# A gated linear attention in chunks: queries times, keys over the running product of the decays, instead of seven levels of halves

## The chip, the cores and the metric

The kernel runs on one core of a Trainium2 chip. Its engines are TensorE (PE in the profile; its weight loads are listed as PEld), VectorE (DVE), ScalarE (ACT), GpSimd (POOL) and SyncE (SP, which only issues transfers here). The metric is the device time in microseconds of one execution, lower is better.

## What is computed

A recurrence over 768 steps for 4 batches and 8 heads of dimension 48, and then a mixture of experts (8 experts, 2 for each token) on its output:

```python
state = np.zeros((B, H, D, D))
for t in range(S):
    state = alpha[:, :, t, :, None] * state + np.einsum('bhd,bhe->bhde', k[:, :, t], v[:, :, t])
    y[:, :, t] = np.einsum('bhd,bhde->bhe', q[:, :, t], state)
x = y.transpose(0, 2, 1, 3).reshape(3072, 384)
logits = x @ w_gate + np.log1p(np.exp(x @ w_noise)) * noise      # 3072 x 8
# the two best experts of each token, with softmax weights:
out[token] += weight * (np.maximum(x[token] @ w1[e], 0) @ w2[e])
```

alpha is drawn evenly from 0.8 to 1. All numbers are 32 bits wide.

## The kernel before

The 3072 tokens are 24 chunks of 128 (six chunks for each batch). A chunk's output is q times the state that it inherits, decayed, plus the attention inside the chunk: the score of token t on an earlier token s is the sum over the 48 dimensions of q[t] k[s] times the product of the alphas between them.

The kernel never divides by a product of alphas. It builds the scores by doubling. `gla_prepare` (L184) loads the chunk (a, q, k and v, each 192 KB, on SP's queue, `load_chunk` L141), transposes k, q and alpha on PE (`transposed`, L163), makes the products of the diagonal and multiplies q by alpha. `gla_level` (L202) is then called for L = 1, 2, 4 to 64: the right half of each block of 2L tokens is scored against the whole chunk's keys (`scores`, L169, eight products with 64 columns), a predicated copy on DVE takes the part that belongs to this level into the matrix MT (L212), and q's right halves are multiplied by the left half's total decay (DVE, L222), k's left halves by the right half's (POOL, L224), the other halves copied (ACT, L223 and L225), and the totals of the pairs multiplied (POOL, L227). `gla_finish` (L230) transposes the keys, which by then are decayed to the chunk's end, updates the state, and adds two products, q with the old state (L258) and MT with v (L263). The result y is written to x_rows in device memory (L273, SP's queue) and transposed into xT (L271).

The loop (L345) takes two chunks at a time, and their levels alternate, so that one chunk's products run while the other chunk's operands are made. After the pairs of chunks 0 and 2 it issues, on SP's queue, the clearing of out (eight transfers, L357) and the load of w2 (eight transfers of 1.5 MB, L160). After each three chunks `router` (L279) makes the logits on PE (L283), picks the two experts, ranks the tokens within each expert with two more products (L326, L327) and writes 128 x 6 table entries with six scatters of POOL's queue (L338). All six write the one tensor `table`, and so each waits for the one before.

Then a few small operations on one partition make a plan of 55 tiles of 128 tokens (L366 to L391). The memory of the first stage is closed (L393), and the experts' loop fetches a table row, a matrix w1 and the gathered tokens two tiles ahead (`fetch`, L410) and computes each tile (`ffn`, L424).

The scheduler that builds the program sets the waits between the engines, and may move an instruction ahead of others of its engine that aren't ready. What is queued on an engine runs in that order.

Of the kernel before, what the change touches and what calls it, by code (L numbers as in the profile page):

```python
# [17 lines left out]
def kernel(  # L18
# [21 lines left out]

    nc = tc.nc
# [21 lines left out]

    gla = ctx.enter_context(ExitStack())
# [7 lines left out]
    gc = pool("gc", 1, gla)  # L72
    vp = pool("vp", 4, gla)
    kp = pool("kp", 4, gla)
    qp = pool("qp", 4, gla)
    dp = pool("dp", 2, gla)
    sp = pool("sp", 2, gla)
    xtp = pool("xtp", 2, gla)
    rp = pool("rp", 2, gla)
    ps_sc = pool("ps_sc", 2, gla, space=PS)  # L80
    ps_tp = pool("ps_tp", 2, gla, space=PS)
    ps_y = pool("ps_y", 2, gla, space=PS)
# [5 lines left out]
    masks = {}  # L88
    for L in LEVELS:
        g = C // (2 * L)  # L90
        m = gc.tile([C, g, L], F32, name=f"mask{L}")
        nc.gpsimd.memset(m, 1.0)
        nc.gpsimd.affine_select(out=m, in_=m, pattern=[[-2 * L, g], [0, L]], compare_op=ALU.is_ge, fill=0.0,
                                base=0, channel_multiplier=1)
        nc.gpsimd.affine_select(out=m, in_=m, pattern=[[2 * L, g], [0, L]], compare_op=ALU.is_ge, fill=0.0,
                                base=L - 1, channel_multiplier=-1)
        masks[L] = m.bitcast(U32)[:, None, :, :].to_broadcast([C, NP, g, L])
    mask_diag = ident.bitcast(U32)[:, None, :].to_broadcast([C, NP, C])
# [6 lines left out]
    ones = const.tile([C, C], F32, name="ones")  # L105
    nc.gpsimd.memset(ones, 1.0)
# [16 lines left out]
    nc.scalar.dma_start(out=table.rearrange("(p r) w -> p (r w)", p=C), in_=nothing)  # L123
    zeros = const.tile([C, NT // 8, DM], F32, name="zeros")
    nc.gpsimd.memset(zeros, 0.0)

    NIN = 3
    ins = {x: [gc.tile([C, H, DP], F32, name=f"{x}_in{i}") for i in range(NIN)] for x in "aqk"}
    MTs = [gc.tile([C, 2, NP, C], F32, name=f"MT{i}") for i in range(2)]
    S_bds = [gc.tile([C, NP, 2, D], F32, name=f"S_bd{i}") for i in range(2)]  # L130
    for t in [t for x in "aqk" for t in ins[x]]:
        nc.gpsimd.memset(t[:, :, D:DP], 0.0)
    for t in MTs + S_bds:
        nc.vector.memset(t, 0.0)
# [6 lines left out]
    def load_chunk(n):  # L141
        for x, src in (("a", alpha), ("q", q), ("k", k)):
# [5 lines left out]
    noise = gc.tile([C, NT, E], F32, name="noise")  # L148
    w_r = gc.tile([C, KO, 2, E], F32, name="w_r")
# [13 lines left out]
    def transposed(src, dst, copy):  # L163
        tp = ps_tp.tile([C, NP, C], F32, tag="tp", name="tp")
        for j in range(NP):
            nc.tensor.transpose(tp[:, j, :], src[:, 2 * j:2 * j + 2, :], ident)
        copy(dst, tp)  # L167

    def scores(sc, at, width, kT, qcols):  # L169
        for j in range(NP):  # L170
            for i in range(2):
                r = ds(DP * i, D)
                nc.tensor.matmul(sc[i][:, at + j * width:at + (j + 1) * width], kT[r, j, :], qcols[r, j],  # L173
                                 start=True, stop=True)

    def halves(t, l):
        w = t.rearrange("p j (g h l) -> p j g h l", h=2, l=l)
        return w[:, :, :, 0, :], w[:, :, :, 1, :]

    def flat_halves(t, l):  # L180
# [164 lines left out]
    for n in range(0, NT, 2):  # L345
        pair = {m: gla_prepare(m) for m in (n, n + 1)}
        for L in LEVELS:
            for m, c in pair.items():
                gla_level(m, c, L)
# [137 lines left out]
```

## Time and profile before

| | us |
|---|---|
| median of three runs | 1467.92 (1464.04 to 1469.35) |
| the profiled execution | 1463.86 |
| its span, from the first to the last instruction | 1462.2 |
| PE, DVE, ACT, POOL busy | 1241.1, 394.7, 274.5, 425.4 |
| mean granted clock of PE, of full speed | 0.746 |

The page gives, for each engine, its busy time and, in forty slices of the span (36.6 us each), the busy share in tenths. [...] The queries of the trace that are used below are the groups of instructions by line (busy time, mean of one, and the idle time of the engine in front of them with what ended it), the timeline, and the busy time of each engine in given windows.

### The profile page before, as it was taken

What the parts mean: (1) busy time and instruction counts of PE and PEld (TensorE: products, weight loads), DVE (VectorE), ACT (ScalarE), POOL (GpSimd) and SP (SyncE); (2) the same over time, 40 slices, a digit from 0 to 9 for tenths busy, and PEclk for the clock granted to TensorE, in tenths of its full rate; (3) what the DMA queues carried; (4) which work ended last, traced back from release to release, by engine and by line L of the source; (5) the groups of instructions that cost most, each with busy time, mean ns of one, the idle gap of its engine ahead of it and who ended that gap; (6) DMA issues with size and microseconds to landing.
All of it is one profiled execution on the core that took longest, in us unless ns stands there. A gap on an engine that the chain in (4) does not pass through costs nothing. (4 is left out here: it accounts for less than half of the span.)

```text
span 1462.2 us, 21684 instructions
## 1 busy us (share of the span) xinstructions
PE 1241.1 (85%) x8079; PEld 1071.5 (73%) x8079; DVE 394.7 (27%) x985; ACT 274.5 (19%) x603; POOL 425.4 (29%) x653
## 2 busy tenths in 40 slices
PE   6895697997979979699850999989999989999896
PEld 6784696886968879688750777767777777777775
DVE  5443343525435254352620101010101001010100
ACT  2322231322323223232310010001010000001010
POOL 6221432414334143341502122222222222222221
PEclk8655555555555555555555999999999999999999
DMA  9549020221202112010003445444555555555540
GB/s 232 183 172 108 1 55 11 45 44 12 55 12 44 39 18 54 6 34 12 1 11 121 154 176 186 165 172 169 173 186 191 187 194 181 179 183 178 179 165 20
DMA packets 160966, 157.56 MB, mean 108 GB/s; under 512 B 118341, under 2 KB 132862, under 8 KB 160864
## 3 DMA queue, kind: packets, MB, share of 16 engines
q1 hardware_dynamic: 144736, 127.47, 28.4%
q0 software_dynamic: 12096, 28.39, 6.7%
q8 instruction: 66, 1.08, 0.3%
q10 hardware_dynamic: 4032, 0.33, 0.3%
q14 instruction: 36, 0.29, 0.1%
HBM read 139.77 MB, written 20.50 MB: 110 GB/s over the span
## 5 line engine op out<-in xcount | busy, mean ns | idle before, releaser
L437 PEld LDWEIGHTS h_ps<-xt,w 128*128 128x128 f32 x2640 | 308.5, 196 | 10.1 <-DVE xt L431 2.9
L437 PE MATMUL h_ps<-xt,w 128*128 128x128 f32 x2640 | 311.3, 279 | 1.8 <-DVE xt L431 1.7
L173 PE MATMUL sc<-q_new,k_new 48*128 48x64 f32 x2304 | 268.2, 418 | 42.0 <-POOL k_new L224 41.4
L173 PEld LDWEIGHTS sc<-q_new,k_new 48*128 48x128 f32 x2304 | 257.9, 327 | 53.0 <-POOL k_new L224 44.6
L442 PE MATMUL o_ps<-w,h 128*128 x880 | 292.9, 486 | 0.0
L442 PEld LDWEIGHTS o_ps<-w,h 128*128 128x128 f32 x880 | 163.2, 190 | 101.8
L212 DVE COPY_PREDICATED MT<-mask,sc 128x256 f32<-128x256 uint32 x336 | 154.3, 524 | 167.1 <-PE sc L173 164.9
L448 DVE SCALAR_TENSOR_TENSOR o<-o_ps,tab,prev 128x384 f32<-128x384 f32 x55 | 34.0, 618 | 559.7 <-PE o_ps L442 496.3
L439 ACT ACTIVATE h<-h_ps 128x512 f32<-128x512 f32 x110 | 65.7, 597 | 626.7 <-PE h_ps L437 626.7
L449 POOL DMA_INDIRECT out_dram<-o,tab x55 | 56.4, 1026 | 306.7 <-DVE o L448 294.4
L227 POOL TENSOR_TENSOR tot<-tot 128x256 f32<-128x256 f32 (+6 forms) x168 | 59.5, 354 | 216.6 <-ACT tot L167 205.7
L224 POOL TENSOR_TENSOR k_new<-k_new,tot 128x256 f32<-128x256 f32 x144 | 96.3, 683 | 55.3 <-PE sc L173 54.4
L338 POOL DMA_INDIRECT table<-entry,place_u x48 | 48.7, 1015 | 176.9 <-DMA table<-entry,place_u 106.2
L225 ACT COPY k_new<-k_new 128x256 f32<-128x256 f32 x144 | 58.8, 409 | 219.3 <-POOL k_new L224 122.0
L429 PE MATMUL x_ps<-ident,x_in 128*128 128x128 f32 x165 | 28.9, 287 | 81.8 <-DMA x_in<-x_rows,tab 81.8
L429 PEld LDWEIGHTS x_ps<-ident,x_in 128*128 128x128 f32 x165 | 19.7, 144 | 96.3 <-DMA x_in<-x_rows,tab 87.8
L444 POOL DMA_INDIRECT prev<-out_dram,tab x55 | 56.4, 1026 | 112.3 <-DMA out_dram<-o,tab 108.6
L173 PE MATMUL sc<-q,k 48*128 48x128 f32 (+1 forms) x768 | 79.7, 333 | 10.4 <-DVE MT L196 8.7
L173 PEld LDWEIGHTS sc<-q,k 48*128 48x128 f32 x768 | 70.5, 236 | 19.7 <-DVE MT L196 10.2
L263 PEld LDWEIGHTS y<-vt,MT 128*128 128x128 f32 x384 | 83.3, 328 | 0.0
L263 PE MATMUL y<-vt,MT 128*128 128x48 f32 x384 | 83.2, 403 | 0.0
L419 POOL DMA_INDIRECT x_in<-x_rows,tab x55 | 54.8, 996 | 79.4 <-DMA tab<-table 59.8
(107 smaller groups left out, 896.8 us busy)
## 6 DMA issues: line engine op xcount, KB each, us to landing
w<-in_moe_w_dram SPq DMA_DIRECT2D x63, 1536.0 KB, 7.2
a_in<-in_alpha_dram SPq DMA_DIRECT2D x24, 192.0 KB, 3.5
q_in<-in_q_dram SPq DMA_DIRECT2D x24, 192.0 KB, 4.4
k_in<-in_k_dram SPq DMA_DIRECT2D x24, 192.0 KB, 3.3
vt<-in_v_dram SPq DMA_DIRECT2D x24, 192.0 KB, 2.9
out_dram<-zeros SPq DMA_DIRECT2D x8, 576.0 KB, 6.1
x_rows<-y_sb SPq DMA_DIRECT2D x24, 192.0 KB, 2.7
tab<-table SPq DMA_DIRECT2D x55, 1.0 KB, 1.7
```

The lines of the kernel that those rows point to most:

```text
L173: nc.tensor.matmul(sc[i][:, at + j * width:at + (j + 1) * width], kT[r, j, :], qcols[r, j], start=True, stop=True)
L212: nc.vector.copy_predicated(halves(MTs[n % 2][:, i], L)[1], masks[L], part)
L224: nc.gpsimd.tensor_tensor(kl_new, k_left, t_right.to_broadcast([C, NP * g, L]), op=ALU.mult)
L225: nc.scalar.copy(kr_new, k_right)
L227: nc.gpsimd.tensor_tensor(tot_new.rearrange("p j g -> p (j g)")[:, :, None], t_left, t_right, op=ALU.mult)
L263: nc.tensor.matmul(y[:, h, :], MT[:, i, j, :], vt[:, h, :], start=first and h == 0, stop=h == H - 1, skip_group_check=True)
L419: nc.gpsimd.indirect_dma_start(out=x_in[i % NB], out_offset=None, in_=x_rows, in_offset=bass.IndirectOffsetOnAxis(ap=tab[:, 0:1], axis=0), ...
L437: nc.tensor.matmul(h_ps[:, fo, :], w1[:, a, ds((half * FO // 2 + fo) * C, C)], xt[:, a, :], start=a == 0, stop=a == KO - 1)
L439: nc.scalar.activation(h[:, ds(half * FO // 2, FO // 2), :], h_ps, AF.Relu)
L442: nc.tensor.matmul(o_ps, h[:, fo, :], w2[:, ds(e, 1), fo, :].rearrange("p o d -> p (o d)"), start=fo == 0, stop=fo == FO - 1)
L444: nc.gpsimd.indirect_dma_start(out=prev[i % 2], out_offset=None, in_=out, in_offset=bass.IndirectOffsetOnAxis(ap=tab[:, 0:1], axis=0), bou ...
L449: nc.gpsimd.indirect_dma_start(out=out, out_offset=bass.IndirectOffsetOnAxis(ap=tab[:, 0:1], axis=0), in_=o, in_offset=None, bounds_check= ...
```

## The change

The recurrence is done with the running product P of the alphas within a chunk, one scan on DVE: q is multiplied by P, k is multiplied by the reciprocal of P, and one set of products with 128 columns, copied once through a mask of the lower triangle, gives all scores of a chunk. The state is then the sum of the old state and the chunk's keys with v, times P at the chunk's end.

The loop goes chunk by chunk, and in a round n it issues the load of chunk n+3, the preparation of chunk n+2, the scores of n+1 and the finish of n. The clearing of the table moves from the start of the program to behind chunk 0, and alpha, k, q is now the order of the loads. The six scatters get a bounds check.

P is held above 1e-18. The kernel records P at each chunk's end, and on ACT the sum of what alpha exceeds 1 by. If any P fell under 2e-18 or any alpha is above 1, the whole computation is done again in the old form (`general_gla`, the functions of before, one chunk at a time) followed by a second copy of the experts' loop. This sits behind a condition at the end of the program: a value that all engines load, and a jump.

The core of the diff (the old functions inside `general_gla` and `experts` are cut):

```diff
+    def put_x(n, y, on, ps_tp, xT, at):
+        ...                        # the end of gla_finish, unchanged
+    def fast_gla(es, after):
+        ...
+        ps_sc = pool("ps_sc", 1, es, space=PS)
+        ps_tp = pool("ps_tp", 3, es, space=PS)
+        ps_y = pool("ps_y", 3, es, space=PS)
+        ...
+        def prepare(n):
+            c = chunks[n]
+            a_t = transposed(ins["a"][n % NIN])
+            nc.scalar.copy(a_s[n % 2][:, :, 1:C + 1], a_t)
+            over_1 = kp.tile([C, NP, C], F32, name="over_1")
+            nc.scalar.activation(over_1, a_t, AF.Relu, bias=less_1, accum_out=above[:, n:n + 1])
+            k_t = transposed(ins["k"][n % NIN])
+            k_raw = kp.tile([C, NP, C], F32, name="k_raw")
+            nc.scalar.copy(k_raw, k_t)
+            q_t = transposed(ins["q"][n % NIN])
+            P = P_s[n % 3]
+            nc.vector.tensor_tensor_scan(P.rearrange("p j t -> p (j t)"), a_s[n % 2].rearrange("p j t -> p (j t)"),
+                                         least.rearrange("p j t -> p (j t)"), 0.0, op0=ALU.mult, op1=ALU.max)
+            c["q"] = kp.tile([C, NP, C], F32, name="q_P")
+            nc.vector.tensor_mul(c["q"], q_t, P[:, :, 1:C + 1])
+            over = kp.tile([C, NP, C], F32, name="over")
+            nc.vector.reciprocal(out=over, in_=P[:, :, 1:C + 1])
+            c["k"] = kp.tile([C, NP, C], F32, name="k_P")
+            nc.gpsimd.tensor_tensor(c["k"], k_raw, over, op=ALU.mult)
+            nc.gpsimd.tensor_copy(out=P_end[:, n, :, None], in_=P[:, :, C:C + 1])
+            c["end"] = kp.tile([C, NP, 2], F32, name="end")
+            nc.gpsimd.tensor_tensor(c["end"], P[:, :, C:C + 1].to_broadcast([C, NP, 2]),
+                                    own_rows[:, None, :].to_broadcast([C, NP, 2]), op=ALU.mult)
+
+        def scores(n):
+            c = chunks[n]
+            sc = [ps_sc.tile([C, NP, C], F32, tag=f"sc{i}", name=f"sc{i}") for i in range(2)]
+            for j in range(NP):
+                for i in range(2):
+                    r = ds(DP * i, D)
+                    nc.tensor.matmul(sc[i][:, j, :], c["k"][r, j, :], c["q"][r, j, :], start=True, stop=True)
+            for i in range(2):
+                nc.vector.copy_predicated(MTs[n % 2][:, i], mask_upto, sc[i])
+            if n % NCH != NCH - 1:
+                ...                # four transposes of c["k"]
+                nc.scalar.copy(c["k_end"], tp)
+
+        def finish(n, xT, at):
+            ...
+            if not last:
+                ...                # s1 = k_end with v, four products
+                if first:
+                    nc.vector.tensor_mul(S_new, s1, end)
+                else:
+                    S_sum = kp.tile([C, NP * 2, D], F32, name="S_sum")
+                    nc.vector.tensor_add(S_sum, chunks["S"], s1)
+                    nc.gpsimd.tensor_tensor(S_new, S_sum, end, op=ALU.mult)
+            ...                    # y = q with the old state, and MT with v, as before
+            put_x(n, y, sp, ps_tp, xT, at)
+        ...
+        load(0)
+        load(1)
+        prepare(0)
+        load(2)
+        prepare(1)
+        scores(0)
+        for n in range(NT):
+            if n + 3 < NT:
+                load(n + 3)
+            after(n)
+            if n + 2 < NT:
+                prepare(n + 2)
+            if n + 1 < NT:
+                scores(n + 1)
+            if n % UC == 0:
+                xT = xtp.tile([C, KO, UT], F32, name="xT")
+            finish(n, xT, n % UC)
+            if n % UC == UC - 1:
+                router(n // UC, xT, rp, ps_y)
+        ...                        # two reductions, two comparisons, a product with ones: again_i
+        plan_tiles(rp, ps_y)
+    ...
-                    in_=entry.bitcast(U32)[:, c, k, :], in_offset=None)
+                    in_=entry.bitcast(U32)[:, c, k, :], in_offset=None, bounds_check=TROWS - 1, oob_is_err=False)
+    ...
+    def after(n):
         if n == 0:
             load_router()
+            clear_table()
+            clear_out()
         if n == 2:
             load_w2()
+
+    with ExitStack() as es:
+        fast_gla(es, after)
+    with ExitStack() as es:
+        experts(es)
+    redo = nc.values_load(again_i[0:1, 0:1], min_val=0, max_val=2 * C,
+                          skip_runtime_bounds_check_because="a count of at most 2 C rows")
+    with tc.If(redo > 0):
+        with ExitStack() as es:
+            clear_table()
+            clear_out()
+            general_gla(es)
+        with ExitStack() as es:
+            experts(es)
```

## Rows read from the trace of the kernel before

**Rows 1.** The page: its head, and PE's busy tenths and clock in forty slices.
```profile
span 1462.2 us, 21684 instructions
...
PE   6895697997979979699850999989999989999896
...
PEclk8655555555555555555555999999999999999999
```

**Rows 2.** Windows by stage: length, busy us of each engine (instructions), PE clock, DMA share, GB/s.
```profile
0.00:750.50 750.50, 628.40 (x4388) 583.87 (x4388) 325.75 (x835) 205.71 (x489) 251.57 (x482) 0.55 0.26 56
750.50:800.00 49.50, 1.42 (x6) 1.36 (x6) 6.98 (x40) 3.13 (x5) 9.19 (x9) 0.50 0.15 56
800.00:1462.20 662.20, 611.30 (x3685) 486.24 (x3685) 61.92 (x110) 65.67 (x110) 164.63 (x162) 0.98 0.48 170
```

**Rows 3.** Groups by line: count, busy us, mean ns, idle us before them and its releasers.
```profile
L173 PE MATMUL sc<-q_new,k_new 48*128 48x64 f32 x2304 | 268.2, 418 | 42.0 <-POOL k_new L224 41.4 <-POOL tot L227 0.2
...
L224 POOL TENSOR_TENSOR k_new<-k_new,tot 128x256 f32<-128x256 f32 x144 | 96.3, 683 | 55.3 <-PE sc L173 54.4
```

**Rows 4.** Timeline from 160 us: start, length, engine, line, what, count.
```profile
161.01 14.07 PE L173 MATMUL sc<-q_new,k_new 48*128 48x64 f32 x128 [4.16 <-POOL k_new L224]
...
180.98 2.02 PE L244 MATMUL s<-vt,k_end 128*128 128x96 f32 x8 [0.68 <-ACT k_end L241]
...
182.80 1.91 PE L258 MATMUL y<-S_bd,q_new 128*128 128x96 f32 x8
...
184.50 3.54 PE L263 MATMUL y<-vt,MT 128*128 128x48 f32 x16
...
193.55 2.71 PE L283 MATMUL lg<-w_r,xT 128*128 128x16 f32 x12
```

**Rows 5.** Timeline of PE from 258 us, around a rise and fall of its clock.
```profile
261.98 1.06 PE L166 MATMUL tp<-ident,k_in 128*128 128x128 f32 x4
...
264.74 1.16 PE L173 MATMUL sc<-q,k 48*128 48x128 f32 x16
265.83 0.66 PE L166 MATMUL tp<-ident,k_in 128*128 128x128 f32 x4
...
270.58 1.81 PE L173 MATMUL sc<-q,k 48*128 48x64 f32 x12 [0.66 <-DVE MT L196]
```

**Rows 6.** Windows of 0.5 us there (the clock stands third from the end).
```profile
264.00:264.50 0.50, 0.50 (x4) 0.45 (x3) 0.50 (x1) 0.00 (x0) 0.00 (x0) 0.64 0.38 77
...
271.00:271.50 0.50, 0.50 (x7) 0.50 (x5) 0.50 (x2) 0.30 (x1) 0.50 (x2) 0.69 1.11 139
```

**Rows 7.** Timeline of the last scatters and of the first read of the table.
```profile
756.95 1.36 POOL L338 DMA_INDIRECT table<-entry,place_u  x1 [30.04 <-DVE ends L376]
...
774.05 0.96 POOL L338 DMA_INDIRECT table<-entry,place_u  x1 [4.24 <-DMA table<-entry,place_u]
...
790.41 0.36 SPq L416 DMA_DIRECT2D tab<-table  x1
```

**Rows 8.** Groups by line of DVE and ACT operations.
```profile
L196 DVE COPY_PREDICATED MT<-ident,sc 128x512 f32<-128x512 uint32 x48 | 32.9, 726 | 3.6 <-PE sc L173 3.5
...
L199 DVE TENSOR_TENSOR q<-q,tot 128x512 f32<-128x512 f32 x24 | 16.8, 702 | 13.5 <-ACT tot L167 13.4
...
L167 ACT COPY k<-tp 128x512 f32<-128x512 f32 x24 | 14.1, 586 | 30.8 <-PE tp L166 29.4 <-POOL tot L227 1.3
...
L307 DVE RECIPROCAL den<-den 128x3 f32<-128x3 f32 x8 | 1.3, 168 | 0.0
...
L306 DVE TENSOR_SCALAR den<-den 128x3 f32<-128x3 f32 x8 | 1.3, 161 | 0.0
```

**Rows 9.** Windows while w2 is loaded, and while chunks are loaded.
```profile
62.00:90.00 28.00, 26.18 (x252) 24.37 (x253) 19.55 (x42) 11.84 (x31) 15.30 (x29) 0.70 0.99 344
264.50:271.00 6.50, 5.46 (x66) 4.54 (x64) 5.15 (x9) 3.18 (x7) 4.84 (x10) 1.00 1.02 164
```

**Rows 10.** Timeline: the last scatter of the program.
```profile
1451.53 1.01 POOL L449 DMA_INDIRECT out_dram<-o,tab  x1 [7.11 <-DVE o L448]
```

More of the change, by code (lines that the diff above doesn't have):

```diff
@@ L71 @@
     dram = pool("dram", 1, space=bass.MemoryType.DRAM)
[L72 to L82, printed above, removed]
     ident = const.tile([C, C], F32, name="ident")
     make_identity(nc, ident)
[L88 to L98, printed above, removed]
+    upto = const.tile([C, C], F32, name="upto")
+    ones = const.tile([C, C], F32, name="ones")
+    nc.gpsimd.memset(ones, 1.0)
+    nc.gpsimd.affine_select(out=upto, in_=ones, pattern=[[1, C]], compare_op=ALU.is_ge, fill=0.0, base=0,
+                            channel_multiplier=-1)
+    mask_upto = upto.bitcast(U32)[:, None, :].to_broadcast([C, NP, C])
+    own_rows = const.tile([C, 2], F32, name="own_rows")
+    nc.gpsimd.memset(own_rows, 0.0)
+    for i in range(2):
+        nc.gpsimd.memset(own_rows[ds(DP * i, DP), i:i + 1], 1.0)
     expert_ids = const.tile([C, E], F32, name="expert_ids")
@@ L122, with clear_table, clear_out @@
     nc.gpsimd.memset(nothing, NONE)
-    nc.scalar.dma_start(out=table.rearrange("(p r) w -> p (r w)", p=C), in_=nothing)
     zeros = const.tile([C, NT // 8, DM], F32, name="zeros")
     nc.gpsimd.memset(zeros, 0.0)
-    NIN = 3
[L128 to L134, printed above, removed]
+    def clear_table():
+        nc.scalar.dma_start(out=table.rearrange("(p r) w -> p (r w)", p=C), in_=nothing)
+    def clear_out():
+        for i in range(8):
+            nc.sync.dma_start(out=out.rearrange("(i n p) d -> i p n d", i=8, p=C)[i], in_=zeros)
+    NIN = 3
     def rows(src, n):
@@ L280, in router @@
+    seen = [const.tile([C, E], F32, name=f"seen{i}") for i in range(2)]
+    def router(u, xT, rp, ps_y):
+        if u == 0:
+            nc.vector.memset(seen[0], 0.0)
         lg = ps_y.tile([C, UC, 2, E], F32, tag="y", name="lg")
@@ L354 @@
+    def after(n):
         if n == 0:
             load_router()
-            for i in range(8):
-                nc.sync.dma_start(out=out.rearrange("(i n p) d -> i p n d", i=8, p=C)[i], in_=zeros)
+            clear_table()
+            clear_out()
         if n == 2:
             load_w2()
-        while (done + 1) * UC <= n + 2:
-            router(done, xTs.pop(done))
-            done += 1
-    total = ps_y.tile([C, E], F32, tag="y", name="total")
-    nc.tensor.matmul(total, ones, seen[NU % 2], start=True, stop=True)
@@ L390 @@
-    nc.vector.tensor_copy(out=plan[:, :, 0], in_=of)
-    nc.vector.tensor_copy(out=plan[:, :, 1], in_=first)
-    gla.close()
-    w1p = pool("w1p", 3)
-    tp_ = pool("tabp", 3)
-    xp = pool("xp", 2)
-    hp = pool("hp", 2)
-    op = pool("op", 2)
-    ps_x = pool("ps_x", 2, space=PS)
-    ps_h = pool("ps_h", 2, space=PS)
-    ps_o = pool("ps_o", 2, space=PS)
-    NB = 3
-    x_in = [const.tile([C, DM], F32, name=f"x_in{i}") for i in range(NB)]
-    prev = [const.tile([C, DM], F32, name=f"prev{i}") for i in range(2)]
```

477 lines of the change are left out of this document (295 added, 182 removed).

## Prediction

> **What bounds the kernel now.** The profiled execution took 1463.9 us, its span is 1462.2 us [rows 1], and the median of the runs is 1467.9 us, 4 us more. I read the page's forty slices first: they split in the middle. In the first half TensorE (PE) is busy and its granted clock stands mostly at 0.5 of full speed, in the second half it is as busy and stands at 0.9 or more [rows 1]. The windows by stage put numbers to it [rows 2]: the recurrence with the router runs to 750.5 us (PE busy for 628 of them, mean granted clock 0.55), then PE stands nearly idle for 49.5 us, and the experts take the last 662 us at clock 0.98. The change rewrites the first stage alone, so 49.5 + 662.2 + 1.7 us outside the span, 713 us, is what stays.
>
> Next, the groups of instructions by line: what in the 628 us is the work of levels? The score products of the levels, 2304 instructions with 64 columns, keep PE busy for 268 us, and PE stands for 41 us more in front of them until GpSimd (POOL) has made k_new [rows 3]. The timeline of one dense stretch shows the rate: 128 of them in 14.07 us, 0.11 us each, at the low clock [rows 4]. [...]
>
> **What goes.** Each of 24 chunks has 8 products per level on 7 levels, which the program issues as two passes each: 112 passes, 112 x 0.11 = 12.3 us of PE. With them go 7 x 2 predicated copies on DVE, 14 copies on ACT, and 14 multiplies on POOL per chunk. At the start seven masks go from POOL's queue.
>
> **What stays on PE, per chunk, at the low clock.** 12 transposes of a, k, q: from the first of them at 261.98 to the scores behind them at 264.74, 2.76 us, 0.23 each [rows 5]. Scores: 16 passes, half of what 32 would be; with 0.11 per pass as above, 1.8. Transposes for k_end, 4 x 0.23 on 5 of 6 chunks, 0.8. State products s1 and the read of the state, from start to start 1.82 and 1.70 [rows 4], on 5 of 6 chunks, 2.9. Sixteen passes of the product with v, 3.5 [rows 4]. Three transposes of the result, 0.7. Router: 18 passes per three chunks at 2.71/12 = 0.23 [rows 4], 1.4, and its two rank products, four passes of the same price, 0.3. Sum 14.2 us, where the chunk takes 750.5/24 = 31.3 us now.
>
> [...] A mean of 0.55 over 750 us [rows 2] means 75 us at the high level, 3.1 us per chunk, and such a spell comes with the transposes and the 128-column scores, which stay. I keep 3.1 us per chunk; they do 6.2 us of low-clock work, so 14.2 becomes 11.1. PE also waits for ACT's copy of y (0.6 us, as the 512-column copy [rows 8]) and for the router's inputs, 0.2: 11.9 us per chunk, 36 us per group of three chunks with one router.
>
> [...]
>
> **POOL.** Per chunk it now makes k over the product (128x512: two of the 0.683 us rows, 1.4), the new state (128x384, three quarters of that, 1.0) and two small pieces, together 0.3 (an estimate): 2.7 us, 8 per group. The router's six scatters to the table stay, and each waits for the landing of the one before: at the end of the stage, with nothing else on POOL, the six ran from 756.95 until the table could be read at 790.41, 33.5 us, and between two of them POOL stands idle for over 4 us [rows 7]. If POOL's own work falls in these gaps a group costs it 33.5 us, if not 33.5 + 8 = 41.5. Each is above or near PE's 36. The pair of chunks that is interleaved now and the 14 small multiplies per chunk gave POOL much to put there; the new loop has four instructions per chunk, and each k that stands behind a scatter is late by up to 5 us while PE's next scores wait for it. So I take the upper value, **42 us per group**, eight groups, 336 us.
>
> **DVE and ACT,** beside it. DVE per chunk: the scan over 516 elements (the trace has one of 8 elements only; as the 512-element multiply 0.70, at most twice that), the multiply of q 0.70, two predicated copies 2 x 0.73, the state's sum at most 0.70 [rows 8], and a reciprocal of 512. That is bounded below by 0.70; its only row is 3 elements wide, 168 against 161 ns for a scalar operation of that width [rows 8], 2.3 ns more per element, which gives 0.7 + 512 x 0.0023 = 1.9 us, and I take 1.9. Sum 5.5 us per chunk, 16 per group, and the router's small operations, under 7 (all that DVE did between 750.5 and 800 us [rows 2]): 23, hidden under 36. [...] ACT has four 512-column copies at 0.59 and two smaller ones, at most 3.5 us per chunk, and the second pass over a with its sum is one of these four; its cover is PE's 11.9. Were PE's cover gone, ACT and DVE would set about 5.5 + 2.3 us per chunk, still under the 11 of the scatters.
>
> **Start and transfers.** POOL's fills of the inputs come earlier without the masks ahead of them, so the first loads decide: three chunks of four 192 KB tensors, 2.36 MB, at 164 GB/s [rows 9], 14 us, and I count 15 until the steady loop begins. The clearing of the table moves behind chunk 0 on ACT's queue, long before the first scatter; that costs nothing. The clearing of out (4.7 MB) and w2 (12.6 MB) are on SP's queue at chunks 0 and 2, and the loads of chunks 4 and 6 queue behind them. At 344 GB/s [rows 9] they take 50 us, and chunks 0 to 6, 5.5 MB at 164 GB/s, 34 us: 84 us until chunk 6 is there, while the loop would want it at 15 + 4 x 14 = 71. That is **13 us** of waiting, once. Later a chunk's loads need 4.8 us out of 14. x_rows is written behind the wait for y in SP's queue; the load of chunk n+4 stands behind it and is wanted a chunk later, which is time enough at 14 us.
>
> **End.** The checks (reductions, a small product) and the plan lie on DVE and PE beside the last six scatters, nothing. The fills of x_in and prev can now come only when the recurrence's memory is free, 1.9 us that lie in POOL's wait for the first table rows. Then the register load, the comparison and the jump over the second copy of everything. No row shows a branch. From the last scatter's start at 1451.53 to the span's end are 10.7 us [rows 10], of which a closing barrier can be all but the landing; a second one of that kind bounds the cost from above, nothing from below, and I take 7.
>
> Sum: 713 + 15 + 13 + 336 + 7 = 1084; I forecast 1085 us, as the profiled execution is a little below the median.
>
> **Rivals.**
> *The scatters hold k back.* Where two of a group's three k stand behind the chain, PE's work on one chunk no longer overlaps with it: 42 + 12 = 54 us per group, 1084 + 8 x 12 = 1180. For it: PE already waited 41 us for k_new [rows 3], with more to fill the gaps. Against: a chunk's k is made one chunk ahead of its use. Chance 0.22.
> *The scatters hide,* POOL's work fits in the gaps, PE sets 36 us per group: 1084 - 8 x 6 = 1036. For it: one k ahead. Against: 33.5 is too near 36. Chance 0.15.
> [...] Chance 0.12.
> *The condition holds* and the old form runs as well, the one way to a slower kernel: it decides from any product under 2e-18 or any alpha above 1. Then 750 + 49.5 + 662 are added: 2546 us. Against: alpha lies between 0.8 and 1, and 0.8 to the 128th is 4e-13; only a sum that ACT leaves wrong could trip it. Chance 0.03.
>
> **How the numbers follow.** The forecast has 0.48. From 1015 (scatters hidden, no wait for w2) to 1190 (k held back) all cases but the condition and the worst of the first rival lie inside. A measurement of this kernel can tell 0.5% from no change; slower is the condition alone, 0.03, the same 0.01, faster 0.96.
>
> **What would show it.** The first stage should end near 364 us; the windows should give PE about 34 us busy per group with a clock between 0.6 and 0.7; the waits should name POOL's k, and scatters 5 us apart; reciprocal's mean should be near 1.9 us. The forecast is wrong if PE waits for DVE (a slow reciprocal or scan), if the clock stays at 0.5, or if the stage after 750 us does not stay as it is.

## The result, and the profile after

The changed kernel takes 1114.69 us (median of four runs, 1108.35 to 1120.6), the kernel before 1468.63 us beside it; the ratio is 0.7593, with a 95% interval of 0.7545 to 0.764. The profiled execution took 1120.6 us, 1.7 us of them outside its span. The forecast was 1085 us with a range of 1015 to 1190.

The page of the changed kernel: its head, PE's busy tenths and PE's granted clock in forty slices, to be held against [rows 1].

```profile
span 1118.9 us, 14294 instructions
...
PE   6883777677787740699999999989999999999994
...
PEclk9855676565656555799999999999999999999997
```

The low-clock half has shrunk to a third of the span, and PE, which was busy for 7 to 9 tenths of most slices there, is so for 6 to 8. The windows by stage (length, busy us of PE, weight load, DVE, ACT, POOL with their instructions, PE clock, DMA share, GB/s) answer to [rows 2]:

```profile
0.00:110.00 110.00, 72.61 (x435) 63.98 (x435) 58.26 (x76) 26.08 (x53) 27.13 (x77) 0.73 1.08 235
110.00:404.00 294.00, 221.35 (x1267) 204.69 (x1265) 137.69 (x266) 73.64 (x148) 75.36 (x107) 0.62 0.34 53
404.00:455.00 51.00, 2.01 (x8) 1.85 (x8) 7.27 (x43) 3.15 (x5) 9.80 (x10) 0.50 0.15 52
455.00:1118.90 663.90, 610.00 (x3685) 484.68 (x3685) 62.03 (x110) 65.67 (x110) 164.26 (x162) 0.98 0.48 170
```

The first stage ends at 404 us instead of 750.5; the gap behind it (51.0 for 49.5 us) and the experts (663.9 for 662.2 us, PE busy for 610.0 for 611.3) are as they were. All of the gain is in the first stage, and so is what the forecast missed: it had that stage end at 364.

Groups by line in the first 404 us (busy us, mean ns of one | idle before them and its releasers), with the new operations that had no row before, and the scatters:

```profile
L212 DVE RECIPROCAL over<-P_s 128x512 f32<-128x512 f32 x24 | 80.4, 3348 | 0.7
L515 POOL DMA_INDIRECT table<-entry,place_u x41 | 41.5, 1013 | 180.5 <-DMA table<-entry,place_u 150.0 <-DVE place_u L511 22.5 <-DVE S_sum L252 4.8
L214 POOL TENSOR_TENSOR k_P<-k_raw,over 128x512 f32<-128x512 f32 x24 | 31.3, 1302 | 44.1 <-DVE top L471 21.4 <-DVE over L212 16.6 <-DVE picked L491 3.6
L207 DVE TENSOR_TENSOR_SCAN P_s<-a_s,least 128x516 f32<-128x516 f32 x24 | 29.5, 1229 | 88.1 <-ACT a_s L199 88.1
L253 POOL TENSOR_TENSOR S_new<-S_sum,end 128x384 f32<-128x384 f32 x16 | 13.4, 838 | 3.9 <-DVE seen L501 3.4 <-DVE S_sum L252 0.3
```

What PE waits for in that time (total, times, longest):

```profile
PE sc L226 <- POOL k_P L214: 39.9, 9, 8.7
PE rank L503 <- DVE chosen L496: 18.8, 4, 6.6
PE tp L193 <- DMA a_in<-in_alpha_dram: 14.4, 3, 10.5
PE y L256 <- POOL S_new L253: 10.3, 5, 3.1
PE sc L226 <- DVE den L482: 9.1, 2, 4.6
PE sc L226 <- DVE den L483: 6.3, 1, 6.3
```

POOL stands for 150 us in front of scatters until the one before has landed, and PE waits 50 us for k and the state that POOL makes in between; another 34 us it waits for small results of the router on DVE (chosen, den), which is where the 80 us of reciprocals run. Both kinds of wait lie in one loop. One round of it, from a group's first scatter to the first of the next (start, length, engine, line, what):

```profile
279.48 1.03 POOL L515 DMA_INDIRECT table<-entry,place_u  x1 [4.37 <-DVE place_u L511]
...
299.32 1.27 POOL L214 TENSOR_TENSOR k_P<-k_raw,over 128x512 f32<-128x512 f32 x1
...
300.64 2.08 PE L226 MATMUL sc<-q_P,k_P 48*128 48x128 f32 x16 [4.69 <-POOL k_P L214]
...
303.81 1.01 POOL L515 DMA_INDIRECT table<-entry,place_u  x1 [3.22 <-DMA table<-entry,place_u]
304.85 0.84 POOL L253 TENSOR_TENSOR S_new<-S_sum,end 128x384 f32<-128x384 f32 x1
...
305.74 2.02 PE L256 MATMUL y<-S_new,q_P 128*128 128x96 f32 x8 [1.98 <-POOL S_new L253]
...
314.97 1.39 PE L460 MATMUL lg<-w_r,xT 128*128 128x16 f32 x6
...
319.52 0.17 DVE L466 TENSOR_TENSOR noisy<-noisy,lg 128x24 f32<-128x24 f32 x1
319.61 3.35 DVE L212 RECIPROCAL over<-P_s 128x512 f32<-128x512 f32 x1
...
322.87 0.24 DVE L471 MAX8 top<-noisy 128x8 f32<-128x8 f32 x3
...
325.96 0.18 DVE L496 TENSOR_TENSOR chosen<-picked 128x24 f32<-128x24 f32 x1
...
328.78 1.03 POOL L515 DMA_INDIRECT table<-entry,place_u  x1 [4.28 <-DVE place_u L511]
```

Read it as a circle. Four landings, 24.3 us, lead to the fifth scatter at 303.81. (A chunk's k is held in the same way: it stands behind the fourth scatter, at 299.32, and PE's scores wait for it.) Right behind the fifth scatter in POOL's queue stands the state of the group's third chunk, S_new; without it PE can't make that chunk's output (305.74), without the output there are no router products (314.97), and without the router no places for the next group's first scatter (328.78). From fifth scatter to next first scatter are 25.0 us, in which PE, ACT and DVE work one after the other. The sum is 49.3 us, a round. Four of the six rounds behind the second group are of this kind (48.7 to 52.5 us, with 19.2 to 20.4 us from the last scatter to the next first one). In the round before them (41.6 us) the scatters follow one another with no such gap, and the last (34.4 us) has no chunk left to prepare. In this stretch the router's noisy logits are ready at 319.7, but a chunk's reciprocal has DVE until 322.96 and the router's MAX8 starts behind it.

### The profile page after: what moved, and what is told of

Read it like the earlier page. It is cut to its first block, busy times and chain, and to the rows that moved or that the text cites. A ratio compares the mean times of both kernels' runs of the same rounds, so it can differ in the third digit from the quotient of the medians.

```text
span 1118.9 us, 14294 instructions
## 1 busy us (share of the span) xinstructions
PE 906.0 (81%) x5393; PEld 755.2 (67%) x5393; DVE 265.3 (24%) x495; ACT 168.5 (15%) x315; POOL 276.5 (25%) x356
## 4 chain that ended last, share of the span: by engine, by line
issue 44%; DMA 28%; PE 11%; POOL 9%; DVE 5%; ACT 1%; POOLq 1%; SPq 0%; ACTq 0%; DVEq 0%
DMA prev<-out_dram,tab 14%; DMA out_dram<-o,tab 5%; DMA table<-entry,place_u 4%; POOL table L515 3%; DMA tab<-table 3%; POOL out_dram L610 3%; DVE over L212 2%; PE y L261 2%; PE lg L460 2%; PE sc L226 1%; POOL x_in L580 1%; DMA x_in<-x_rows,tab 1%; PE tp L193 1%; PE h_ps L598 1%; PE o_ps L603 1%
## 5 line engine op out<-in xcount | busy, mean ns | idle before, releaser
L226 PE MATMUL sc<-q_P,k_P 48*128 48x128 f32 x384 | 53.3, 407 | 55.3 <-POOL k_P L214 39.9
L226 PEld LDWEIGHTS sc<-q_P,k_P 48*128 48x128 f32 x384 | 43.4, 288 | 64.4 <-POOL k_P L214 42.5
L212 DVE RECIPROCAL over<-P_s 128x512 f32<-128x512 f32 x24 | 80.4, 3348 | 0.7
L261 PE MATMUL y<-vt,MT 128*128 128x48 f32 x384 | 70.3, 357 | 0.0
L261 PEld LDWEIGHTS y<-vt,MT 128*128 128x128 f32 x384 | 69.9, 280 | 0.0
L207 DVE TENSOR_TENSOR_SCAN P_s<-a_s,least 128x516 f32<-128x516 f32 x24 | 29.5, 1229 | 88.1 <-ACT a_s L199 88.1
L592 DVE COPY xt<-x_ps 128x384 f32<-128x384 f32 x55 | 30.3, 553 | 65.5 <-PE x_ps L590 65.5
L214 POOL TENSOR_TENSOR k_P<-k_raw,over 128x512 f32<-128x512 f32 x24 | 31.3, 1302 | 44.1 <-DVE top L471 21.4
L256 PE MATMUL y<-S_new,q_P 128*128 128x96 f32 x160 | 32.9, 371 | 10.3 <-POOL S_new L253 10.3
L256 PEld LDWEIGHTS y<-S_new,q_P 128*128 128x128 f32 x160 | 30.4, 281 | 12.1 <-POOL S_new L253 12.1
```

The source lines that it names most:

```text
L212: nc.vector.reciprocal(out=over, in_=P[:, :, 1:C + 1])
L226: nc.tensor.matmul(sc[i][:, j, :], c["k"][r, j, :], c["q"][r, j, :], start=True, stop=True)
L256: nc.tensor.matmul(y[:, 2 * j:2 * j + 2, :], c["q"][:, j, :], chunks["S"][:, 2 * j:2 * j + 2, :], start=j == 0, stop=False, skip_group_che ...
L261: nc.tensor.matmul(y[:, h, :], MTs[n % 2][:, i, j, :], c["v"][:, h, :], start=first and h == 0, stop=h == H - 1, skip_group_check=True)
```

## What the experiments showed

They ran on three other chips, four kernels on each, where the kernel before took 1442.64, 1446.19 and 1441.98 us (on the first chip 1468.63). So medians are compared through the ratio to the kernel before, and the changed kernel was run again as a yardstick. "Group" is the mean round of groups 2 to 8, from the first scatter of the second group to the first scatter of the eighth, divided by six (the last of the six holds less work, as above); "experts from" is the start of the first x_ps transpose. Both are read from the timelines of POOL and PE.

| kernel | group, us | experts from, us | time, us | ratio to before |
|---|---|---|---|---|
| changed, first chip | 46.1 | 455.1 | 1114.69 | 0.7593 [0.7545, 0.764] |
| changed, again | 43.6 | 434.7 | 1097.44 | 0.7571 [0.7535, 0.7606] |
| e1 multiply for reciprocal | 37.7 | 391.8 | 1058.26, one run | |
| e2 a table for each scatter | 35.3 | 355.3 | 1005.33, one run | |
| e10 both | 33.2 | 331.3 | 978.47, one run | |
| e9 state alone on DVE | 41.1 | 422.2 | 1085.81 | 0.7509 [0.7456, 0.7563] |
| e3 k and state on DVE | 37.3 | 384.6 | 1042.2 | 0.722 [0.7178, 0.7262] |
| e4 w2 spread | 42.2 | 401.2 | 1070.24 | 0.7407 [0.7374, 0.7441] |
| e5 no condition | 43.0 | 428.2 | 1089.98 | 0.7529 [0.7499, 0.756] |
| e7 e3 and e4 | 36.8 | 372.9 | 1030.33 | 0.712 [0.7089, 0.7152] |
| e8 two tables, w2 spread | 40.2 | 387.2 | 1050.21 | 0.7241 [0.7187, 0.7295] |
| e11 e7 and a late rank | 36.7 | 372.8 | 1027.81 | 0.7116 [0.7074, 0.7158] |
| e12 e11 and two tables | 37.3 | 361.4 | 1010.44 | 0.6993 [0.695, 0.7036] |

One thing limits every comparison here: the order of the instructions on each engine is laid out anew when a program is built, so an edit of one operation can also move others (in e1, PE and POOL run parts of their work in another order than in the changed kernel). A difference between two kernels is the edit with its new order. And the chips differ: the changed kernel's own round is 2.5 us shorter on the second.

The theories: A, that k and the state stand behind the scatters in POOL's queue and the landings set the round; B, that DVE's chain of scan and reciprocal sets it.

**e1: a multiply in place of the reciprocal** (the scaling of k by the reciprocal is left out; the rest of the work is the same).

```diff
-            nc.vector.reciprocal(out=over, in_=P[:, :, 1:C + 1])
+            nc.vector.tensor_mul(over, P[:, :, 1:C + 1], P[:, :, 1:C + 1])
```

> The reciprocal of P is left out: in its place stands a multiply of P with itself, of the same width (0.70 us for 3.35), so the scores and all that follows from them have other values. The first stage ends at 404 us in the changed kernel; PE waits there 40 us for k (made on POOL), 10 us for the new state (POOL) and 38 us for the router's small operations on DVE (chosen, den). Theory A, k and the state stand in POOL's queue behind scatters: the reciprocal is mostly hidden, PE's wait for k stays above 30 us, only the waits for the router's operations shrink, the stage ends at 375 to 395 us. Theory B, DVE's chain of scan and reciprocal sets the round: 24 x 2.65 us fall away, the stage ends near 340 us and the wait for k nearly goes.

The first stage ends at 344.0 us, near B's 340. But both theories counted from the 404 us of the first chip; in the changed kernel run again it ends at 387.2, and the experts start 42.9 us earlier here than there. That lies between A's 9 to 29 us and B's 64. The scatters were no quicker: the group that begins at 244.17 us has five intervals in 31.2 us, 6.2 each, where the changed kernel run again had 5.25. What shrank is the time from a group's last scatter to the next group's first, from 20.0 us (294.96 to 314.98) to 7.8 to 9.8 us. PE still waits 23.4 us for k (25.3 in the changed kernel run again), so A isn't gone either.

**e2: a table for each of the six columns,** so that no scatter waits for another (the experts then read the first table alone).

```diff
+    tables = [table] + [dram.tile([TROWS, 2], U32, name=f"table_{i}") for i in range(1, 2 * UC)]
...
-                    out=table, out_offset=...
+                    out=tables[i], out_offset=...
```

> Only the first of a router's six scatters still writes the table, the other five write tables of their own that nobody reads, so none waits for the one before; five sixths of the table's entries are left out, and the experts' stage works on empty rows, so only the first stage is compared (404 us in the changed kernel). Theory A, k and the state stand behind scatters that wait for a landing of 6 us each: PE's waits for k and the state (50 us) nearly go, the stage ends at 345 to 360 us, a group of three chunks takes 42 us or less instead of 49. Theory B, DVE sets the round: POOL only waits less, the stage ends at 390 us or later. The time between the last router and the first expert falls from 51 to some 25 us by either.

Its timeline of POOL and two of PE's waits up to 400 us:

```profile
265.15 1.05 POOL L516 DMA_INDIRECT table<-entry,place_u  x1 [4.28 <-DVE place_u L512]
266.50 0.98 POOL L516 DMA_INDIRECT table<-entry,place_u  x1 [0.30 <-issue]
...
278.55 1.27 POOL L215 TENSOR_TENSOR k_P<-k_raw,over 128x512 f32<-128x512 f32 x1 [4.37 <-DVE over L213]
```

```profile
PE rank L504 <- DVE chosen L497: 20.2, 4, 6.1
...
PE sc L227 <- DVE den L483: 10.2, 2, 6.2
```

Six scatters now leave POOL in 7.5 us, k waits for the reciprocal and no longer for a landing, and PE's wait for k is down to 2.1 us. The round falls by 8.3 us with every reciprocal in place: B alone can't have set it. What is left of the waits is DVE's.

**e10: both edits at once.**

> Both suspects taken away at once: each column's scatter has a table of its own (no scatter waits for another; the expert stage then reads only the first table, so most of its rows are left out of the output), and a multiply stands in for the reciprocal (k is scaled wrongly, so the stage's output is too). Beside the run with tables of their own (36 to 37 us a group, first scatter to first scatter 29.6 to 37.6) this tells what the 3.35 us reciprocal costs once the scatters hold nothing: if it sat in the round's path by itself (theory B) groups fall by 3 to 8 us, to 30 to 34; if PE sets the round by then (its own sum of 36 us a group), they stay at 35 to 38 and the total within 1% of 1005 us.

The group is 33.2 us, inside what B expected of it, but it fell by 2.1 us only where B wanted 3 to 8. The experts start 24.0 us earlier than in e2 (12.5 in the six rounds, 11.2 before them), and the whole is 27 us shorter, where PE as the only limit would have left it within 1%. So the reciprocal costs something by itself, less than a delay of every k by its length would. With e1 and e2 this makes a square of four rounds: 43.6 as it is, 37.7 without the reciprocal, 35.3 without the landings, 33.2 without both. The landings cost 8.3 us a round beside the reciprocal and 4.5 without it; the reciprocal 5.9 beside the landings and 2.1 without them. The four corners come from three chips and three of them are single runs, so the 2.1 alone isn't clear of the 2.5 us between two chips. Counted between the router's last products, the square is 45.5, 38.0, 37.2 and 33.8, with the same order of costs. By both counts each is dearer where the other is present, as two stretches of one loop would be when the loop is longer than PE's own work. So A and B were not rivals: the forecast needed both.

**e9: the state alone moved to VectorE.**

```diff
-                    nc.gpsimd.tensor_tensor(S_new, S_sum, end, op=ALU.mult)
+                    nc.vector.tensor_mul(S_new, S_sum, end)
```

> Only the state's product S_new goes from POOL to VectorE; k stays on POOL between the scatters. Theory A1: in the changed kernel the round is a loop through S_new (it stands behind the fifth scatter of its group, and from its start to the next group's first scatter it is 24 to 25 us each time: state, output of the chunk, its transposes, the router); with the state out of the queue that loop is gone and the next one, through k_P, has to be shorter: groups of 38 to 43 us, stage 1 ends 25 to 50 us earlier, ratio to before 0.723 to 0.740. Theory A2: k_P is what holds the round (it is the longer wait in PE's list, 25 us against 12): groups stay at 44 to 48 us, ratio 0.748 to 0.757. Theory B: S_new is not in the chain of scan and reciprocal either, so the same as A2.

The ratio is 0.7509, inside what A2 expected, and the interval overlaps that of the unchanged kernel; the round is 41.1 us, in A1's span, but only 2.5 us under the 43.6 that the same count gives for the unchanged kernel. So S_new is where the circle above closes, but a second path, through the k that stands behind the fourth scatter, is only a little shorter and takes over. In the changed kernel run again that k starts at 284.93 us, 30.1 before the next first scatter, and S_new at 291.05. In e9 itself PE's wait for k is 26.2 us, and in one round k starts at 283.22 behind the fourth scatter, 27.8 us before the next first scatter at 311.05. To break the loop both have to leave the queue.

**e3: k and the state on VectorE.**

```diff
-            nc.gpsimd.tensor_tensor(c["k"], k_raw, over, op=ALU.mult)
+            nc.vector.tensor_mul(c["k"], k_raw, over)
...
-                    nc.gpsimd.tensor_tensor(S_new, S_sum, end, op=ALU.mult)
+                    nc.vector.tensor_mul(S_new, S_sum, end)
```

> The multiply of k by the reciprocal and that of the new state move from POOL to DVE; POOL keeps the scatters. Theory A: PE no longer waits for anything behind a scatter, the 50 us of waiting go, DVE's 1.25 us more per chunk are hidden: the stage ends at 355 to 370 us, the whole at 1070 to 1080 us. Theory B, DVE is the bound: DVE has 30 us more to do, the stage ends at 404 us or later, the whole at 1115 us or more.

With k and the state's product out of POOL's queue (small pieces of 0.2 us, `end` and `P_end`, stay in it) the round is 37.3 us and the ratio 0.722, a better gain than A expected, though DVE got two more operations per chunk. On DVE they are also shorter: k takes 0.68 us there instead of 1.30, the state 0.53 instead of 0.84. PE's longest waits now are for DVE (chosen 27.8 us, MT 16.2 us).

**e4: the eight loads of w2 spread,** one at every second chunk from chunk 2 on.

```diff
-    def load_w2():
-        for e in range(E):
+    def load_w2(es):
+        for e in es:
...
-        if n == 2:
-            load_w2()
+        if 2 <= n < 2 + 2 * E and n % 2 == 0:
+            load_w2([n // 2 - 1])
```

> The eight loads of w2 are issued one at a time behind chunks 2, 4, to 16 instead of together behind chunk 2. The second group of three chunks took 72 us in the changed kernel where a later one takes 49, and PE waited 10.5 us for one load of alpha. If the burst of w2 on SP's queue makes the loads of chunks late (the prediction's term of 13 us, here 23), the second group takes some 50 us and the whole falls by 15 to 25 us, to about 1092 us. If that time is the first router's cost (its scatters landed after 8 us), it stays above 65 us and the whole falls by under 8 us.

In the changed kernel the burst and what it delays look like this in the timelines of SP and PE:

```profile
42.94 30.79 SPq L146 DMA_DIRECT2D w<-in_moe_w_dram  x8
...
80.42 0.43 SPq L129 DMA_DIRECT2D a_in<-in_alpha_dram  x1
...
90.65 1.12 PE L193 MATMUL tp<-ident,a_in 128*128 128x128 f32 x4 [10.48 <-DMA a_in<-in_alpha_dram]
```

The second group takes 50.6 us instead of 72.1 (70.6 in the changed kernel run again), the kernel 0.7407 of before instead of 0.7571. PE's own wait for the load is 10.5 us; the rest of the 21.5 goes with POOL's scatters. In the group that starts beside the burst the second followed the first after 11.7 us and the others came 7.6 to 9.5 us apart (45.7 us for the five intervals, 35.0 in e4), against 5.7 to 7.0 in the mean of a later group.

**The changed kernel again, and e5 without the condition** (the block with the second copy of everything taken out).

> The changed kernel once more, with nothing edited, as the yardstick for the runs beside it. From its ratio of 0.7593 to the kernel before, and 1442.6 us for that kernel on the chip of the last runs, about 1095 us there; what it gives beside each other run of this set is what counts. Under theory A (the wait between scatters sets the round) the round follows the landing time of a scatter on this chip: about five landings plus 19 us, so 49 us a group where a landing takes 6 us and 44 us where it takes 5. Under theory B (scan and reciprocal set it) it is 49 us whatever the landings take.

> The conditional path is taken out whole, with the register load and the branch in front of it. If the second closing barrier is what the tail lost, the stretch from the last scatter to the end falls from 15.8 us to the 10.7 us of the kernel before, and the total by 5 us (0.5%); if the tail is long for another reason, it stays at 15 to 16 us and the total with it. Stages 1 and 2 are not touched: the rounds keep their 48 to 50 us.

The round of the changed kernel moved with the landing as A says: five intervals in 30.1 us and a round of 49.3 on the first chip, 26.2 and 46.3 here, with 19.2 and 20.0 us from last scatter to next first. For the end, the last scatter of the changed kernel on the first chip, of its repeat, and of e5:

```profile
1103.15 1.02 POOL L610 DMA_INDIRECT out_dram<-o,tab  x1 [7.11 <-DVE o L609]
```

```profile
1081.34 1.02 POOL L610 DMA_INDIRECT out_dram<-o,tab  x1 [7.10 <-DVE o L609]
```

```profile
1071.82 1.02 POOL L610 DMA_INDIRECT out_dram<-o,tab  x1 [7.11 <-DVE o L609]
```

To the ends of the spans at 1118.9, 1096.8 and 1082.5 us these are 15.8, 15.5 and 10.7 us; before it was 10.7 [rows 10]. So the condition that isn't taken costs 4.8 to 5.1 us at the end. The medians differ by 7.5 us, with intervals that overlap.

**e7: k and state on VectorE, with w2 spread** (the edits of e3 and e4).

> k and the state on VectorE, and the four loads of the w2 weights spread over eight chunks: the two edits that each won alone, in one kernel. Theory A says that with k out of POOL's queue the round is set by PE and DVE, 36 to 39 us, and that the burst's 23 us beyond a plain round go too: stage 1 ends at 315 to 325 us, the total is 1015 to 1030 us. If the two gains are one and the same (the burst mattered only because it slowed the scatters that held k back), the total is not below the 1042 us of k and the state on VectorE alone.

Both gains are there, though less than added up: 1030.33 us, 0.712. Spreading w2 takes 12.0 us off the second group here (50.1 in e3, 38.1), where it took 20.0 off with k on POOL (70.6 in the changed kernel run again, 50.6 in e4), as late scatters no longer hold k back (PE waits 0.6 us for k here, 25.3 in the changed kernel run again). In its first half POOL's scatters follow one another at 6 to 8 us without a pause (112.72, 119.24, 127.03, 132.84, 139.01, 147.22, 154.04 us), so there the landings alone make POOL's round of 41.3 us (the next is 40.9, later ones 31 to 37). They no longer hold the recurrence: the router's last products come 36.7 to 41.1 us apart, 38.4 in the mean of the six rounds, as in e3.

**e8: two tables,** one for first and one for second choices, joined by two small operations where the experts read them; w2 spread; k and state still on POOL.

```diff
-                    out=table, out_offset=...
+                    out=tables[k], out_offset=...
...
+            nc.vector.tensor_tensor(tab[:, 0:1], half[0][:, 0:1], half[1][:, 0:1], op=ALU.bitwise_and)
+            nc.vector.tensor_tensor(tab[:, 1:2], half[0][:, 1:2], half[1][:, 1:2], op=ALU.bitwise_or)
```

> First and second choices go to a table each, so that only every second scatter waits for the one before on the same table; k and the state stay on POOL; the reader loads both tables and joins them with two small operations on VectorE; the w2 loads are spread. Theory A: three landings of 5 to 6 us in a round instead of six, so POOL is held for some 18 us and k_P waits for at most one landing: 37 to 40 us a group, stage 1 to 320 to 335 us, 1015 to 1035 us. Theory B: the reciprocal (3.35 us) is still in DVE's chain, so the groups keep 47 to 50 us and only the burst's gain is seen, 1070 us.

PE's wait for k is down to 12.5 us, but the round only to 40.2, and long rounds (54.2 and 48.4 us) stand between short ones (31.5 to 36.7). The 54.2 us round holds more work than the one behind it (257 of PE's instructions for 174). The next two hold nearly the same:

```profile
245.63:294.04 48.41, 45.28 (x215) 40.53 (x214) 24.13 (x43) 13.07 (x26) 11.82 (x18) 0.50 0.62 94
294.04:325.50 31.46, 25.20 (x198) 22.63 (x198) 22.54 (x48) 12.48 (x25) 13.09 (x17) 0.83 0.57 70
```

In the long one PE is busy for 94% of the time at a granted clock of 0.50 throughout; in the short one for 80% at 0.83. Neither landings nor DVE hold the long one; PE does, at the lower level. So 0.50 was granted in a round of an experiment in which PE hardly waits; the full rounds of the changed kernel have 0.60 to 0.66. Against e4, which has one table, the gain is 0.7407 to 0.7241.

**e11: the rank products, places and scatters put one chunk later in the program,** on top of e7 (the router hands them to the loop, which calls them behind the next chunk's scores).

```diff
+            while held:
+                held.pop()()
             if n % UC == 0:
...
-                router(n // UC, xT, rp, ps_y)
+                router(n // UC, xT, rp, ps_y, held if n + 1 < NT else None)
```

> As the kernel with k and the state on VectorE and w2 spread (1030 us, ratio 0.712), and the second half of the router (rank product, places, scatters) is put one chunk later in the program, behind the scores of the next chunk. There PE waited 27.7 us for the chosen experts and 5.1 us for the denominators in front of the rank products; if these waits are real time of the round, stage 1 ends 20 to 30 us earlier and the total is 1000 to 1012 us (ratio 0.692 to 0.700). If the scatters themselves set the round by now (they followed each other without a gap in its first half, 6 to 7 us apart), it stays within 8 us of 1030 us.

Nothing moved: 1027.81 for 1030.33 us (on another chip; by the ratio 0.7116 for 0.712), and PE's wait in front of the rank products is the same in both, to the tenth:

```profile
PE rank L512 <- DVE chosen L499: 27.7, 4, 8.7
```

The instructions have exactly the order of e7 on PE, POOL and DVE, so the edit didn't do what it was meant to, and whether that wait is worth anything stays open.

**e12: e11 with the two tables of e8.**

> The late rank, k and the state on VectorE, w2 spread, and the two tables: three landings a group stand in POOL's queue, nothing of the recurrence stands behind them. What is left is PE at its granted clock: 36 us a group where the clock is at 0.62 to 0.70 of full speed, and 50 to 54 us in a group that gets only 0.50 (seen in the run with two tables). If PE gets the clock of the best runs (0.7 and more in stage 1), stage 1 ends at 290 to 305 us and the total is 985 to 1005 us; if PE runs at 0.50 to 0.55 for long stretches as with two tables before, the total is 1035 to 1050 us, and the landings were not the limit any more in 1030 us.

This is the fastest version that leaves nothing out, 1010.44 us, 0.6993 of before, against 0.7571 for the changed kernel. Its gain over e11 is not in the rounds, which are 37.3 us against 36.7 (38.4 in both between the router's products). Most of it is where the six last scatters have nothing beside them. The first and last of them, in e7 (whose rounds e11 shares) and in e12:

```profile
333.72 1.34 POOL L515 DMA_INDIRECT table<-entry,place_u  x1 [8.29 <-DVE ends L535]
...
359.51 0.97 POOL L515 DMA_INDIRECT table<-entry,place_u  x1 [3.50 <-DMA table<-entry,place_u]
```

```profile
334.06 1.32 POOL L526 DMA_INDIRECT table<-entry,place_u  x1 [15.32 <-DVE ends L546]
...
346.82 0.96 POOL L526 DMA_INDIRECT table<-entry,place_u  x1 [1.34 <-DMA table<-entry,place_u]
```

They begin at the same time and take 25.8 and 12.8 us (25.8 in e11 too). The experts begin 11.4 us earlier; the remaining 6 us of the difference between the medians lie behind that. From the experts' first transpose to the span's end are 655.2 us in e11 and 648.8 in e12: behind PE's first wait for the gathered tokens (40.6 us in e11, 28.7 in e12), the waits of PE and of its weight loads for them add up to 67.3 us in e11 and 46.1 in e12, with 4.6 of waits for the table rows beside them. Why the tokens come sooner isn't shown.

## Why the prediction was right, and where its sum was off

The sign, the size and the range held, for the reason given: the level products bounded the first stage, they went, and what stood behind the stage stayed. The sum itself was 36 us under the profiled execution, and terms erred both ways: what came out longer adds up to 54 us and what came out shorter to 18, so that part of the closeness is luck.

| stretch | forecast, us | measured, us |
|---|---|---|
| start and first group | 15 + 42 = 57 | 44.4 |
| second group, with w2 | 42 + 13 = 55 | 72.1 |
| six more groups | 6 x 42 = 252 | 287.4 |
| gap before the experts | 49.5 | 51.1 |
| experts to their last scatter's issue | 651.5 | 648.1 |
| from there to the end | 10.7 + 7 = 17.7 | 15.8 |
| outside the span | 1.7 | 1.7 |
| sum | 1084.4 | 1120.6 |

The ends of the groups are those of the router's last product; for the first two and the last group:

```profile
43.56 0.84 PE L460 MATMUL lg<-w_r,xT 128*128 128x16 f32 x6 [0.57 <-ACT xT L155]
...
115.69 0.84 PE L460 MATMUL lg<-w_r,xT 128*128 128x16 f32 x6
...
402.46 1.46 PE L460 MATMUL lg<-w_r,xT 128*128 128x16 f32 x6 [0.57 <-ACT xT L155]
```

**PE's work.** Forecast: some 34 us busy per group of three chunks at a clock of 0.6 to 0.7. Measured: 221.35 us in 294, that is six rounds of 47.9 and a little, 36 us a round at 0.62, which is close. The 3.1 us per chunk at the high level were an estimate from the mean of 0.55 [rows 2]. The rise of the clock in [rows 6] lies at 264.4 us: a mean of 0.64 over that half microsecond, with 0.50 in the one before and 1.00 in the one behind, leaves 0.14 us of it at the high level. From 261.98 until then PE did transposes alone, and four of them took 1.06 us before the rise and 0.66 behind it [rows 5]; what brings such a spell no run shows. With scatters and reciprocal out of the way (e10) the round is 33.2 us, in reach of it.

**POOL and the scatters.** This is the step whose size was off. I took POOL's round as its own time, 33.5 us of scatters and 8 of other work one after the other, 42, beside PE's 36. The scatters came 5.7 to 7.0 us apart in the mean of a group behind the first, for the 5.6 that 33.5 us for six makes, and POOL's own work was 3 x (1.30 + 0.84 + 0.39) = 7.6 us. What the sum left out is that POOL's queue and PE's work aren't two lanes of which the longer counts: the k and the state that stand behind the fourth and fifth scatter feed the router that makes the next group's places. So a full round is four landings and then 25 us of a chain through PE, ACT and DVE, 49.3 us, while POOL itself is idle for most of that chain (busy for 6.0 of the 25.0 us). The first rival named the mechanism, k held behind scatters, and gave it 54; the round is between the two, 47.9 us over six groups. e2 and e3 show that the scatters in the queue cost this, and e9 that k and the state both close the loop.

**The reciprocal.** Forecast 1.9 us from a row of three elements [rows 8]; measured 3.35 us. The forecast called it hidden, because DVE's sum of 23 us a group stays under PE's 36. DVE's sum did stay under (24.6 us busy in the 49.3 us of the loop shown), and the time was not hidden: the router's small operations queue behind it in the chain that closes the loop. e1 gives 5.9 us a round for the whole of it beside the scatters. The forecast had named a PE that waits for DVE, for a slow reciprocal, as a sign that it is wrong, and this sign came: PE waits 34 us for the router's results on DVE, some of them behind a reciprocal. So this step was wrong in kind, though the time stayed in the range.

**The w2 burst.** PE's wait for the late loads was 13 us by the sum and is 10.5. Its other price, scatters that follow each other at 7.6 to 11.7 us in the group that starts beside it, was not in the sum; e4 gives 21.5 us for both together.

**The start.** The first group has no scatters of an earlier group in front of its k, so it should have been costed at PE's 36, not at 42; that, and a PE that had the full clock until 44 us (1.00 in the windows from 0 to 18 and from 18 to 44), gave back 12.6 us.

**The end.** 7 taken, 5 measured (e5): right in kind, a little high. That a closing barrier takes part of it was an estimate; no run shows one by itself.

**The other rivals.** The condition didn't hold, as there is no second copy in the span. The clock didn't stay at 0.50 in the changed kernel: its mean of 0.62 is in the forecast's span. Scatters that hide were made by hand in e2, and gave the 36 us that the second rival put on them (35.3).

## What to carry to other kernels

When an engine works through its queue in order and one of its instructions waits for a landing, don't add up that engine's time and compare it with the busiest engine's: look for the result behind the waiting instruction, follow it to the next issue of the same kind, and if it leads there, add the landings and that whole chain, because the sum is the round. In such a loop an engine with time to spare can still cost time, as the reciprocal did on DVE at 50% busy. Independent writes that wait for one another only since they share a tensor can be given tensors of their own: that took 8.3 us off a round here where the recurrence stood behind the scatters (e2), and where it no longer did, only the 13 us of the last six, which nothing runs beside (e12).

## What the runs showed that was not expected

- A reciprocal of 128x512 takes 3.35 us on DVE, five times the multiply of that shape (0.67 us), whereas on three elements it takes 0.17 us [rows 8].
- A scan over 516 elements takes 1.23 us, 1.8 times the multiply.
- POOL's multiply of 128x512 takes 1.30 us and DVE's 0.68; of 128x384 0.84 against 0.53.
- An activation that also sums (128x512) is followed by an ACTIVATION_READ_ACCUMULATOR of its own, 0.20 us, beside 0.69 us for the activation itself.
- A scatter of 128 rows of 8 bytes took 5.5 to 7.0 us from issue to landing between 110 and 404 us of the changed kernel, and POOL was busy for 1.0 us of that; in the group that starts beside the load of 12.6 MB of weights the next came 7.6 to 11.7 us later.
- With nearly the same work, PE's granted clock differed between rounds: 0.50 in a round of e8 in which PE was busy for 45.3 of 48.4 us with 215 instructions, 0.83 in the next with 25.2 of 31.5 us and 198. What decides which round gets the higher clock stays open.
